# A compact attention state on the quarters of TensorE, with y sharing the scores' buffer

## The chip, the cores and the metric

The kernel runs on one core of one Trainium2 chip. The metric is the device time of one execution in microseconds (us); the median of several executions is given with its range. One run of the kernel before took 829.36 us at a granted clock of 0.849, where the ten others in its rounds took 724.08 to 726.72 us at 0.992 to 0.995; that run was in the slow state, and every run below is in the fast state unless it is marked otherwise. e1 to e4, e5 to e8 and e9 to e11 are three sets of rounds on three chips, each with its own runs of the kernel before. "Correct" means that the output was compared with the reference on the chip and agreed.

The engines are TensorE (PE in the profile; PEld are its weight loads), VectorE (DVE), ScalarE (ACT), GpSimd (POOL) and SyncE (SP), which here issues most transfers.

## The reference

A retention block (a linear attention with a decaying state) feeds a feed-forward block.

```python
# q, k, v: (4, 8, 768, 64): batch, heads, sequence, head width
gamma = 1.0 - 2.0 ** (-5.0 - np.arange(H))          # one decay for each head
for t in range(S):
    state = gamma * state + outer(k[t], v[t])       # (B, H, 64, 64)
    y[t] = (q[t] @ state) / sqrt(64)
x = y.transpose(0, 2, 1, 3).reshape(3072, 512)      # tokens x (head, width)
h = x @ w_in                                        # 512 -> 2048
out = (h * sigmoid(1.702 * h)) @ w_out              # 2048 -> 512
```

The weights come as float64. The kernel fetches them as raw 32-bit pairs and narrows them to f32 itself, on ACT and DVE, while it already computes.

## The kernel before

The sequence is cut into chunks of 128 tokens: 6 for each of 4 batch entries, 24 in all. `load` and `turn` bring q and k in and transpose them, `attend` makes the scores of a chunk and masks them, `finish` makes y and updates the state. The pieces of later chunks are woven between the dense matmuls of the feed-forward block. P is 128, H is 8 heads, HP is 4 pairs of heads, D is 64, NC is 6.

```python
state = [const.tile([P, HP, P], F32, name=f"state{i}") for i in range(2)]   # cleared at the start
...
w1v = moe_w_in.bitcast(U32).rearrange("(c p) (f two) -> p c f two", p=P, two=2)
SRC = [w1v[:, 2 * h:2 * h + 2, 2 * p * P:2 * (p + 1) * P] for p in range(NP) for h in range(2)] + ...
def fetch():                       # one transfer of 512 KB onto all 128 partitions
    ...
    sp.dma_start(x.rearrange("p (c f) two -> p c f two", c=2) if i < NFF else x, SRC[i])
...
def attend(j):
    p = ps_a.tile([P, 2, HP, P], F32, name="pa")          # ps_a: one buffer of two PSUM banks
    for hp in range(HP):
        for i in range(2):
            r = slice(i * D, (i + 1) * D)
            pe.matmul(p[:, i, hp, :], KT[j][r, hp, :], QT[j][r, hp, :], start=True, stop=True)
    for i in range(2):
        dve.tensor_mul(AT[j][:, i], p[:, i], mask[:, i])

def finish(j):
    c = j % NC
    old, new = state[c % 2], state[(c + 1) % 2]
    ...
    y = ps.tile([P, HP, P], F32, name="py", tag="att")    # "att": two buffers of one bank
    if c:
        for hp in range(HP):                              # two heads at once, block-diagonal
            pe.matmul(y[:, hp, :], old[:, hp, :], qt[:, hp, :], ...)
    for hp in range(HP):
        for i in range(2):                                # left half, right half, left, right
            pe.matmul(y[i * D:(i + 1) * D, hp, :], vn[:, 2 * hp + i, :], a[:, i, hp, :], ...)
    dve.tensor_mul(x[...], y, rowd)                       # eviction of y
    ...
    for hp in range(HP):
        pe.matmul(u[:, hp, :], kd[...], vn[...], start=True, stop=True)    # k times v of two heads
    for i in range(2):
        r = slice(i * D, (i + 1) * D)
        ...                                               # c == 0: copy
        pool.tensor_mul(new[r, :, r], old[r, :, r], cold[r, 2 * H:, None].to_broadcast([D, HP, D]))
        dve.tensor_add(new[r, :, r], new[r, :, r], u[r, :, r])
```

A state tile holds, for each pair of heads, a 128x128 matrix with one head's 64x64 state in the upper left and the other's in the lower right. The other two quarters are zero, and PE multiplies them too: the records of the state matmuls are 128*128 (L247, 1.05 us for 8 records in chunk 8).

## Time and profile before

| | before |
|---|---|
| time, median of 3 runs | 724.99 us (724.62 to 725.17) |
| span of the profiled run, mean granted clock | 722.5 us, 0.994 |
| state matmuls, all 20 chunks (groups by shape) | 14.8 + 7.6 us of PE |
| value matmuls, all 24 chunks (groups by shape) | 17.5 + 10.1 us of PE |
| from a first state start to the first value start, dense chunk | 0.984 us |

Read the engine row first: it says that PE has almost no free time. Then read the slices, which say where the little free time lies (the first two of 40, 36 us). The lines themselves stand in the prediction, with the readings that it draws from them. In the attention of one chunk, PE does scores (pa), then dense work while DVE masks them, then state and value matmuls (both into py), then the update (pu).

### The profile page before, as it was taken

The page shows a single profiled execution, that of the slowest core. Times are in us where ns is not written, and L with a number is a line of the kernel's source. Part 1 is how long each engine was busy: PE and PEld are TensorE (multiplying, and loading weights), DVE is VectorE, ACT ScalarE, POOL GpSimd, SP SyncE. Part 2 cuts the span into 40 slices and gives each one's busy share as a digit, 9 for nine tenths or more (in the row PEclk, how much of TensorE's full clock was granted, in tenths as well). Part 3 has the DMA queues.
Part 4 walks back from the last instruction along what each step waited for, and adds up shares of the span by engine and source line. Part 5 has one row for each costly group of instructions (what it writes and reads, how often), then busy time and mean ns, then how long its engine had stood idle before and what let it go on. Part 6 is the DMA issues. An engine that isn't in the chain of part 4 may idle for free.

```text
span 722.5 us, 9662 instructions
## 1 busy us (share of the span) xinstructions
PE 705.4 (98%) x3776; PEld 588.5 (81%) x3776; DVE 373.2 (52%) x542; ACT 126.7 (18%) x197; POOL 125.7 (17%) x115
## 2 busy tenths in 40 slices
PE   5799999999999999999999999999999999999997
PEld 4688885447888888888888888888888888888886
DVE  4888889993612822443743353553345373244251
ACT  2313323221000001331000332000233000133100
POOL 2241001000464403000333000123100140200030
PEclk9899999999999999999999999999999999999999
DMA  9995333420012324101334200324300320100001
GB/s 255 232 199 145 132 132 114 147 35 11 15 45 40 73 49 103 31 1 16 74 59 87 59 1 8 73 46 86 67 0 2 63 54 1 44 0 1 15 0 44
DMA packets 142765, 46.28 MB, mean 64 GB/s; under 512 B 129920, under 2 KB 136576, under 8 KB 142720
## 3 DMA queue, kind: packets, MB, share of 16 engines
q1 hardware_dynamic: 135504, 39.10, 23.8%
q10 hardware_dynamic: 7216, 6.57, 2.9%
q8 instruction: 30, 0.49, 0.3%
q14 instruction: 15, 0.12, 0.1%
HBM read 39.33 MB, written 6.29 MB: 63 GB/s over the span
## 4 chain that ended last, share of the span: by engine, by line
PE 92%; DVE 5%; DMA 1%; ACT 1%; issue 0%; SPq 0%; ACTq 0%
PE pd L403 38%; PE px L352 15%; PE py L352 11%; PE ph L313 8%; PE ph L300 7%; PE py L251 3%; PE pa L234 3%; PE pu L264 3%; PE py L247 2%; DMA q_in<-in_q_dram 1%; PE pt L217 1%; DVE W L342 1%; DVE G L342 1%; DVE W L343 1%; DVE G L343 1%; ACT W L181 0%
## 5 line engine op out<-in xcount | busy, mean ns | idle before, releaser
L403 PE MATMUL pd<-W,G 128*128 128x256 f32 x1120 | 250.3, 381 | 0.4 <-DVE G L343 0.3
L403 PEld LDWEIGHTS pd<-W,G 128*128 128x128 f32 x1120 | 210.1, 190 | 30.8 <-DVE G L343 1.2
L352 PE MATMUL px<-X,W 128*128 128x256 f32 x512 | 119.0, 379 | 0.0
L352 PEld LDWEIGHTS px<-X,W 128*128 128x128 f32 x512 | 97.3, 190 | 13.2
L352 PE MATMUL py<-X,W 128*128 128x256 f32 x384 | 90.7, 379 | 0.0
L352 PEld LDWEIGHTS py<-X,W 128*128 128x128 f32 x384 | 73.0, 190 | 9.9
L300 PE MATMUL ph<-X,W 128*128 128x256 f32 x256 | 58.2, 382 | 0.0
L225 POOL TENSOR_TENSOR kd<-kn_in,cold 128x512 f32<-128x512 f32 x13 | 13.6, 1042 | 242.0 <-PE pu L264 199.0
L313 PE MATMUL ph<-W,W 128*128 128x512 f32 x128 | 55.1, 592 | 0.0
L300 PEld LDWEIGHTS ph<-X,W 128*128 128x128 f32 x256 | 47.5, 190 | 6.7 <-DVE X L255 0.2
L313 PEld LDWEIGHTS ph<-W,W 128*128 128x128 f32 x128 | 24.3, 190 | 30.2 <-issue 29.2
L344 POOL TENSOR_TENSOR G<-G 128x512 f32<-128x512 f32 x20 | 28.9, 1444 | 113.1 <-DVE G L343 111.7
L237 DVE TENSOR_TENSOR at<-pa,mask 128x512 f32<-128x512 f32 x32 | 20.6, 684 | 45.5 <-PE pa L234 45.5
L281 DVE TENSOR_TENSOR G<-G,sg 128x512 f32<-128x512 f32 x48 | 33.0, 688 | 13.7 <-ACT sg L279 13.7
L279 ACT ACTIVATE sg<-G 128x512 f32<-128x512 f32 x48 | 30.3, 630 | 50.9 <-DVE G L362 30.6
L279 ACT ACTIVATE sg<-ph 128x512 f32<-128x512 f32 x32 | 19.1, 598 | 104.7 <-PE ph L300 56.2
L403 PE MATMUL pd<-W,W 128*128 128x256 f32 x160 | 35.6, 380 | 0.4 <-DVE W L343 0.3
L403 PEld LDWEIGHTS pd<-W,W 128*128 128x128 f32 x160 | 30.2, 190 | 5.6 <-DVE W L343 1.2
L271 POOL TENSOR_TENSOR state<-state,cold 64x256 f32<-64x256 f32 x32 | 25.6, 800 | 44.0 <-DVE state L269 24.8
L255 DVE TENSOR_TENSOR X<-py,rowd 128x512 f32<-128x512 f32 x20 | 13.8, 688 | 33.3 <-PE py L251 33.3
L390 ACT ACTIVATE u<-pd 128x512 f32<-128x512 f32 x6 | 3.6, 597 | 155.1 <-PE pd L403 155.1
L362 DVE TENSOR_TENSOR G<-py,p 128x512 f32<-128x512 f32 x16 | 11.1, 691 | 37.8 <-PE py L352 37.8
(96 smaller groups left out, 682.1 us busy)
## 6 DMA issues: line engine op xcount, KB each, us to landing
v_in<-in_v_dram SPq DMA_DIRECT2D x24, 256.0 KB, 3.9
W<-in_moe_w_in_dram SPq DMA_DIRECT2D x12, 512.0 KB, 5.1
out_dram<-o ACTq DMA_DIRECT2D x24, 256.0 KB, 2.4
kn_in<-in_k_dram SPq DMA_DIRECT2D x21, 256.0 KB, 4.1
W<-in_moe_w_out_dram SPq DMA_DIRECT2D x10, 512.0 KB, 3.7
q_sq<-in_q_dram SPq DMA_DIRECT2D x256, 16.0 KB, 1.8
k_sq<-in_k_dram SPq DMA_DIRECT2D x256, 16.0 KB, 1.8
G<-in_moe_w_out_dram SPq DMA_DIRECT2D x6, 512.0 KB, 3.8
```

The lines of the kernel that those rows point to most:

```text
L234: pe.matmul(p[:, i, hp, :], KT[j][r, hp, :], QT[j][r, hp, :], start=True, stop=True)
L237: dve.tensor_mul(AT[j][:, i], p[:, i], mask[:, i])
L251: pe.matmul(y[i * D:(i + 1) * D, hp, :], vn[:, 2 * hp + i, :], a[:, i, hp, :], start=(not c and hp == 0), stop=(hp == HP - 1), skip_group_ ...
L264: pe.matmul(u[:, hp, :], kd[:, h, :].rearrange("p i d -> p (i d)"), vn[:, h, :].rearrange("p i d -> p (i d)"), start=True, stop=True)
L271: pool.tensor_mul(new[r, :, r], old[r, :, r], cold[r, 2 * H:, None].to_broadcast([D, HP, D]))
L279: act.activation(s, h, AF.Sigmoid, scale=1.702)
L281: dve.tensor_mul(g, h[:, i], s[:, i])
L300: pe.matmul(h[:, ab], w, X[:, 2 * half + c // 2, c % 2, :], start=(ab == 0 and c == 0), stop=(c == 3), skip_group_check=True)
L313: pe.matmul(h, w, X1[:, c // 2:4:2, c % 2, :], start=(c == 0), stop=(c == 3))
L344: pool.tensor_sub(a[1], a[1], a[0])
L352: pe.matmul(acc[:, u, :], W1[:, 2 * d + u, sa, c, :], X[:, sb, c, :], start=(start and u == 0 and c == 0), stop=(stop and c == 1), skip_gr ...
L403: pe.matmul(p0[:, n, :], g1(m, p, sa)[:, n * P:(n + 1) * P], W2[:, sb, p, :], start=(new and p == 0 and n == 0), stop=(last and p == NP - ...
```

## The change

The intent: store only the 64x64 states that are not zero, so that a state tile is half as wide, and multiply each head on its own quarter of the 128x128 array, four heads at a time. y then lies in two banks of PSUM (the memory that TensorE writes its results to), one for each half of the array's rows. That two banks are needed for this is not shown: no run here lets both row halves write one bank. y takes the buffer of the scores, in turn with them. Three things follow. The heads that share a partition half of y change, so the rows of the first weight are needed in another order, and each of its fetches becomes two, one for each half of the partitions. The value matmuls come in another order. The decay of a state becomes one GpSimd instruction instead of two.

```diff
-    state = [const.tile([P, HP, P], F32, name=f"state{i}") for i in range(2)]
+    state = [const.tile([P, HP, D], F32, name=f"state{i}") for i in range(2)]
...
-    w1v = moe_w_in.bitcast(U32).rearrange("(c p) (f two) -> p c f two", p=P, two=2)
+    w1v = moe_w_in.bitcast(U32).rearrange("(o c r d) (f two) -> c r d o f two", o=2, c=2, d=D, two=2)
...
-    SRC = [w1v[:, 2 * h:2 * h + 2, 2 * p * P:2 * (p + 1) * P] for p in range(NP) for h in range(2)] \
+    SRC = [[w1v[c, h, :, :, 2 * p * P:2 * (p + 1) * P] for c in range(2)] for p in range(NP) for h in range(2)] \
...
-            sp.dma_start(x.rearrange("p (c f) two -> p c f two", c=2) if i < NFF else x, SRC[i])
+            if i < NFF:
+                for c in range(2):
+                    sp.dma_start(x[c * D:(c + 1) * D].rearrange("p (o f) two -> p o f two", o=2), SRC[i][c])
+            else:
+                sp.dma_start(x, SRC[i])
...
-        p = ps_a.tile([P, 2, HP, P], F32, name="pa")
+        p = ps_a.tile([P, 2, HP, P], F32, name="pa", tag="pa")
...
-        y = ps.tile([P, HP, P], F32, name="py", tag="att")
+        y = ps_a.tile([P, 2, HP, P], F32, name="py", tag="pa")
+        where = [(y[s % 2 * D:(s % 2 + 1) * D, r, s // 2, :], s, r) for s in range(HP) for r in range(2)]
         if c:
-            for hp in range(HP):
-                pe.matmul(y[:, hp, :], old[:, hp, :], qt[:, hp, :], start=(hp == 0), stop=False,
-                          skip_group_check=True)
-        for hp in range(HP):
-            for i in range(2):
-                pe.matmul(y[i * D:(i + 1) * D, hp, :], vn[:, 2 * hp + i, :], a[:, i, hp, :],
-                          start=(not c and hp == 0), stop=(hp == HP - 1), skip_group_check=True)
+            for out, s, r in where:
+                k = slice(r * D, (r + 1) * D)
+                pe.matmul(out, old[k, s, :], qt[k, s, :], start=(s < 2), stop=False, skip_group_check=True)
+        for out, s, r in where:
+            pe.matmul(out, vn[:, 2 * s + r, :], a[:, r, s, :], start=(not c and s < 2), stop=(s >= 2),
+                      skip_group_check=True)
...
+        if c:
+            pool.tensor_mul(new, old, cold[:, 2 * H:, None].to_broadcast([P, HP, D]))
         for i in range(2):
             r = slice(i * D, (i + 1) * D)
             if c == 0:
-                dve.tensor_copy(new[r, :, r], u[r, :, r])
+                dve.tensor_copy(new[r], u[r, :, r])
             else:
-                pool.tensor_mul(new[r, :, r], old[r, :, r],
-                                cold[r, 2 * H:, None].to_broadcast([D, HP, D]))
-                dve.tensor_add(new[r, :, r], new[r, :, r], u[r, :, r])
+                dve.tensor_add(new[r], new[r], u[r, :, r])
...
-    for t in state:
-        dve.memset(t, 0.0)
```

The cuts leave out only the eviction's new slices and the loads of the row decays in the new order.

More of the change, by code (lines that the diff above doesn't have):

```diff
@@ L243, in finish @@
         vn, a, qt = QKV.pop(("v", j)), AT.pop(j), QT.pop(j)
-        y = ps.tile([P, HP, P], F32, name="py", tag="att")
+        y = ps_a.tile([P, 2, HP, P], F32, name="py", tag="pa")
+        where = [(y[s % 2 * D:(s % 2 + 1) * D, r, s // 2, :], s, r) for s in range(HP) for r in range(2)]
         if c:
-            for hp in range(HP):
-                pe.matmul(y[:, hp, :], old[:, hp, :], qt[:, hp, :], start=(hp == 0), stop=False,
-                          skip_group_check=True)
-        for hp in range(HP):
-            for i in range(2):
-                pe.matmul(y[i * D:(i + 1) * D, hp, :], vn[:, 2 * hp + i, :], a[:, i, hp, :],
-                          start=(not c and hp == 0), stop=(hp == HP - 1), skip_group_check=True)
+            for out, s, r in where:
[4 more added lines that the diff above has]
+                      skip_group_check=True)
         half, t0 = divmod(j % CB * P, TH)
         x = X1 if j // CB == 1 else X
-        dve.tensor_mul(x[:, 2 * half:2 * half + 2, :, t0:t0 + P].rearrange("p s c t -> p (s c) t"), y, rowd)
+        dve.tensor_mul(x[:, 2 * half:2 * half + 2, :, t0:t0 + P], y[:, :, 0:2, :],
+                       rowd.rearrange("p (r o) t -> p r o t", r=2))
         if j + 2 < 2 * CB:
@@ L435 @@
     act.dma_start(cold, col_decay)
-    for s in range(2):
-        act.dma_start(
-            rowd[s * D:(s + 1) * D],
-            bass.AP(tensor=row_decay.tensor, offset=row_decay.offset + s * P,
-                    ap=[[0, D], [2 * P, HP], [1, P]]),
-        )
+    for c in range(2):
+        for r in range(2):
+            act.dma_start(
+                rowd[c * D:(c + 1) * D, 2 * r:2 * r + 2],
+                bass.AP(tensor=row_decay.tensor, offset=row_decay.offset + (2 * c + r) * P,
+                        ap=[[0, D], [4 * P, 2], [1, P]]))
     load(0)
```

## The prediction

> **What bounds the kernel now.** I read the engine table and the 40 slices first, then the chain that ended last, then the groups by shape, and then the timeline around one chunk of the attention (a chunk is 128 tokens of one batch entry; there are 24).
>
> ```profile
> span 722.5 us, 9662 instructions
> PE 705.4 (98%) x3776; PEld 588.5 (81%) x3776; DVE 373.2 (52%) x542; ACT 126.7 (18%) x197; POOL 125.7 (17%) x115
> PE   5799999999999999999999999999999999999997
> PE 92%; DVE 5%; DMA 1%; ACT 1%; issue 0%; SPq 0%; ACTq 0%
> ```
>
> TensorE (PE) is busy in 98% of the span and carries 92% of the chain that ended last. Only the first two slices (36 us) have room. From about 47 us on, everything that takes time out of PE's stream takes it out of the whole, and everything off PE counts only where PE waits for it. DVE and POOL, at 52% and 17%, are no bound.
>
> The timeline of PE around chunk 8, in the middle of a dense stage (columns: start us, length us, engine, line, what, shapes, count):
>
> ```profile
> 225.28 1.16 PE L234 MATMUL pa<-qT,kT 64*128 64x128 f32 x16
> 226.37 3.72 PE L403 MATMUL pd<-W,G 128*128 128x256 f32 x16
> 229.93 1.05 PE L247 MATMUL py<-qT,state 128*128 128x128 f32 x8
> 230.92 1.09 PE L251 MATMUL py<-at,v_in 128*64 128x128 f32 x16
> 231.94 1.16 PE L264 MATMUL pu<-v_in,kd 128*128 128x128 f32 x8
> 232.94 1.25 PE L403 MATMUL pd<-W,G 128*128 128x256 f32 x5
> ```
>
> Each f32 matmul of the program leaves two records, so the 4 state matmuls (L247) are 8 records. Their pace: the group lasts 1.05 us, one record 275 ns (median), so (1.05 - 0.275)/7 = 0.111 us from start to start. The scores (L234) and the value matmuls (L251), which fill half the array each, have 16 records in 1.16 and 1.09 us: twice as many in the same time. The record starts show why: two of them, in different halves, start 7 ns apart, and such pairs follow each other at 109 to 112 ns. So halves do run side by side.
>
> The record starts also show what a change of shape costs. Dense to scores: 310 ns between the last dense start and the first score, against 216 ns between dense records, so 94 ns extra. State to value: 205 ns instead of 112, and 160 ns instead of 109 after the first pair, so 93 + 51 = 144 ns extra. Dense to state costs nothing (216 ns, both are 128*128).
>
> [...]93 to 94 ns extra at a change, pairs 7 ns apart. [...]no run here has shown four quarters at once yet. [...]the second record of the first matmul starts about 0.2 us (at the start of a group) or 0.1 us after the first record of the second matmul.
>
> **The change part by part.**
>
> 1. State matmuls. Removed: 4 of 128*128 per chunk, half of whose weights are zeros of the block-diagonal state (8 records). Added: 8 of 64*64, on four quarters in turn (16 records). From the first state start to the first value start is now 0.984 us in every dense chunk. After, if quarters run four at a time as halves run two at a time: four rounds. The first waits for its mode change, the second comes 0.160 us later (I take the 64-column value group as model), the third and fourth 0.109 us later each, and the value group 0.205 us after that: 0.160 + 0.109 + 0.109 + 0.205 = 0.583 us. Before it there is now a mode change: +0.094 us. Saved per chunk: 0.984 - 0.583 - 0.094 = 0.307 us. There are 20 chunks with a state (24 less the 4 first ones of a sequence).
>
> 2. A new wait. y moves into the buffer of the scores (one buffer of two banks), so the state matmuls can no longer start before DVE has read both halves of the scores. Before, only the value matmuls waited for that. I compared, per chunk, the end of the second mask multiplication (L237) with the first state start. In 12 of the 20 there is slack (0.38 us in one, over 2.1 us in ten, 3.5 us in chunk 1). In 8 there is none:
>
> ```profile
> 74.34 1.27 DVE L237 TENSOR_TENSOR G<-pa,mask 128x512 f32<-128x512 f32 x2
> 74.91 1.05 PE L247 MATMUL py<-G,state 128*128 128x128 f32 x8
> 75.89 1.09 PE L251 MATMUL py<-G,v_in 128*64 128x128 f32 x16
> ...
> 243.50 1.28 DVE L237 TENSOR_TENSOR at<-pa,mask 128x512 f32<-128x512 f32 x2
> 244.59 1.05 PE L247 MATMUL py<-qT,state 128*128 128x128 f32 x8
> 245.57 1.09 PE L251 MATMUL py<-at,v_in 128*64 128x128 f32 x16
> ```
>
> Chunk 5 (above): the mask ends at 75.61, 0.70 us after the state group began. With 0.05 us to release, the state starts at 75.66 and the value group at 75.66 + 0.583 = 76.24 instead of 75.89: 0.35 us lost. Chunk 7 (0.47 us short): 0.12 lost. Chunks 9, 13, 17, 21 (0.19 us short each; 9 is shown): value group at 244.78 + 0.05 + 0.583 = 245.41 instead of 245.57: still 0.15 saved each. Chunks 2 and 3 (0.13 and 0.37 short): 0.30 and 0.06 saved. Chunk 1 lies at 24 to 28 us, where DVE's weight conversion ends later than PE's work: I count 0.
>
> Sum: 11 chunks x 0.307 = 3.4; 4 x 0.15 = 0.6; chunks 2 and 3, 0.36; chunks 5 and 7, -0.47. Together 3.9 us saved.
>
> 3. Value matmuls. Their number and shape stay, their order changes: from left half, right half, left, right to left, left, right, right. If PE can pass a waiting matmul of the busy half, nothing changes. If it stops at the head of its queue, 8 matmuls need 5 slots of two records instead of 4: about 2 x 0.109 = 0.22 us more per chunk, over 24 chunks 5.2 us.
>
> 4. Off the path. POOL decays the state with one 128x256 instruction instead of two of 64x256 (32 took 25.6 us; by the number of columns I expect half), DVE's eviction of y keeps its 512 elements a partition (0.69 us), two clears of 0.49 us go. The next scores now wait for the eviction of y; its end lies 0.28 us ahead of the next scores in chunk 0 and over 3 us in all others. All of that is hidden.
>
> 5. Transfers. Each of the 16 fetches of the first weight is two of half the size. Only in the first 30 us do they matter, where queued loads wait for earlier ones; the bytes are the same. I allow 1 us either way.
>
> **The rivals.**
>
> A. The value matmuls lose their pairing (part 3): 3.9 saved less 5.2 lost, about 726.[...] Against it: in the trace the second matmul does start ahead of the first one's second record. I give it 0.3.
>
> B. Quarters run only two at a time: eight rounds, 0.160 + 6 x 0.109 + 0.205 = 1.02 us plus 0.094, so 0.13 us lost per chunk instead of 0.307 saved. With the waits of part 2 some 4 to 5 us lost, about 729. For it: nothing in this trace has four at once. Against it: row halves and column halves each pair here. I give it 0.1.
>
> C. The new wait for the buffer takes more than part 2 says, because DVE's order shifts, or the start of the kernel, where DVE is full, gets longer: 724 to 726. The order of instructions of the changed program keeps the mask multiplications, evictions and conversions in their places, against it. I give it 0.1.
>
> D. All is hidden or gained as written: 721.1.
>
> **The range.** The main line gives 725.0 - 3.9 = 721.1. Weighing A, B and C in, I move the prediction to 722.0, with 718.8 to 727.0 as the range. Two per cent are 14.5 us. The state matmuls, all told, take 14.8 + 7.6 = 22.4 us of PE in the groups by shape; even halving them would not give 14.5 us, and no rival loses as much. So within 2% has 0.97, faster 0.01, slower 0.02.
>
> **What would show it.** Part 1: 16 state records on quarters in about 0.65 us, four starting within some 25 ns, and 0.58 us from the first state start to the first value start in chunks with slack (0.98 before). If two at a time, 1.0 us. Part 2: PE idle ahead of the state group, released by the mask multiplication, in chunks 5, 7, 9, 13, 17, 21 and nowhere else after 50 us. Part 3: the value group of chunk 8 lasts 1.02 us to the next group; 1.24 would be rival A. Part 4: POOL's state line at about 13 us in all. Part 5: the first dense matmuls still begin at about 29 us. The prediction fails if either pairing assumption is wrong, or if the first 50 us move by more than 1 us.

## The result, and the profile after

The changed kernel is correct and takes 726.2 us (median of 4 runs, 725.46 to 727.38), against 725.08 us for the kernel before in the same rounds (4 runs, 724.62 to 727.03). The ratio is 1.0012, with a 95% interval of 0.9989 to 1.0035: the same by the 2% rule. In a later set of rounds it took 726.3 us (5 runs) against 725.86 us (9 runs), ratio 1.0008 (0.9994 to 1.0022). A ratio here is the mean time of one kernel's fast runs over the mean of the other's in the same rounds, so it is not quite the ratio of the medians quoted beside it. The range of the prediction held, but its main line (a gain of 3.9 us) did not come: there is no gain at all.

The engine table, the slices of PE and the chain that ended last, in the page of the changed kernel:

```profile
span 724.9 us, 9986 instructions
PE 701.1 (97%) x3936; PEld 578.3 (80%) x3936; DVE 371.6 (51%) x540; ACT 126.9 (18%) x197; POOL 110.3 (15%) x99
PE   5599999999999999999999999999999999999997
PE 76%; DVE 10%; SPq 7%; DMA 4%; issue 2%; ACT 1%; POOL 0%; ACTq 0%; DVEq 0%
```

PE is busy for 4.3 us less than before (705.4 to 701.1), and the span is still 2.3 us longer (722.54 to 724.88): PE stands idle for 6.7 us more. The second slice, 7 before and 5 now, says where to look: at the start. The chain has lost 16 points of PE, but that is not a new bound. At chunk 9 PE now waits 0.17 us for a mask, and the chain goes off there through DVE into the loads that DVE waited for long before; all that time PE was busy. In e6 and e7 below, where that wait is gone, the chain is PE's again, with 91% and 90%.

The timeline of PE around chunk 8 (start us, length us, engine, line, what, shapes, count), then around chunk 9, where the brackets show the idle time ahead of a group and what ended it:

```profile
229.80 1.16 PE L239 MATMUL pa<-qT,kT 64*128 64x128 f32 x16
230.89 3.72 PE L411 MATMUL pd<-W,G 128*128 128x256 f32 x16
234.54 0.67 PE L256 MATMUL py<-qT,state 64*64 64x128 f32 x16
235.14 1.14 PE L258 MATMUL py<-at,v_in 128*64 128x128 f32 x16
236.21 1.16 PE L272 MATMUL pu<-v_in,kd 128*128 128x128 f32 x8
```

```profile
249.19 0.67 PE L256 MATMUL py<-qT,state 64*64 64x128 f32 x16 [0.17 <-DVE at L242]
249.79 1.15 PE L258 MATMUL py<-at,v_in 128*64 128x128 f32 x16
250.86 1.16 PE L272 MATMUL pu<-v_in,kd 128*128 128x128 f32 x8
```

The state group is down from 1.05 to 0.67 us with twice as many records: four quarters do run at once. The next two things are small and new. The value group takes 1.14 to 1.15 us instead of 1.09, and 1.07 us pass from its start to the start of the update, instead of 1.02. And chunk 9 waits for DVE.

The timeline of PE in the start, first of the kernel before, then of the changed one (the transposes pt are those of q of chunk 2, the state group is chunk 1's, ph are the first dense matmuls):

```profile
16.01 1.16 PE L234 MATMUL pa<-G 64*128 64x128 f32 x16
21.57 1.09 PE L217 MATMUL pt<-ident,q_in 128*128 128x128 f32 x4 [4.41 <-DMA q_in<-in_q_dram]
24.25 2.08 PE L247 MATMUL py<-G,state 128*128 128x128 f32 x8 [0.46 <-ACT G L218]
...
29.32 3.72 PE L300 MATMUL ph<-X,W 128*128 128x256 f32 x16
```

```profile
17.38 1.16 PE L239 MATMUL pa<-G 64*128 64x128 f32 x16
26.79 1.12 PE L222 MATMUL pt<-ident,q_in 128*128 128x128 f32 x4 [8.24 <-DMA q_in<-in_q_dram]
...
33.93 3.62 PE L308 MATMUL ph<-X,W 128*128 128x256 f32 x16
```

Chunk 1's scores end within 1.4 us of where they ended before; then PE waits 8.24 us for q of chunk 2 instead of 4.41. The load of q is the same. It was issued later (17.80 us instead of 12.98), because it stands in the queue behind the fetches of the first weight, and the dense matmuls begin 4.6 us later.

The same place as the transfers see it. In the transfer view of the first 60 us, GB/s is what was moved in each of 40 slices of 1.5 us. The line under it is the fetches of the first weight: how many, KB each, median us from issue to landing. First the kernel before, then the changed one:

```profile
GB/s 0 126 255 184 214 336 237 219 316 385 389 391 351 233 300 286 215 228 243 4 8 242 395 286 218 218 217 169 0 106 355 338 254 166 166 177 370 176 0 0
...
W<-in_moe_w_in_dram SPq DMA_DIRECT2D x10, 512.0 KB, 5.1
```

```profile
GB/s 0 155 247 208 219 229 206 218 220 223 234 243 232 239 240 222 206 203 194 214 204 229 185 186 239 249 220 197 143 148 3 0 87 258 232 203 208 202 113 258
...
W<-in_moe_w_in_dram SPq DMA_DIRECT2D x20, 256.0 KB, 6.5
```

From 13.5 to 18 us the kernel before moves 385 to 391 GB/s. The changed one never gets over 258. Half as many bytes take longer to land (6.5 us instead of 5.1). In the records of single packets, a 2 KB packet of these fetches took 84 to 87 ns (median) before and 142 to 147 ns after.

The whole balance, from the starts of the state groups in the two traces:

| stretch of the span | before, us | after, us | change |
|---|---|---|---|
| start to the state matmuls of chunk 4 | 59.38 | 63.65 | +4.27 |
| chunk 4 to chunk 8 | 170.55 | 170.89 | +0.34 |
| chunk 8 to chunk 23 (dense) | 382.02 | 379.92 | -2.10 |
| chunk 23 to the end | 110.59 | 110.42 | -0.17 |
| span | 722.54 | 724.88 | +2.34 |

So the matmuls gained, but less than predicted, and the start lost more than that. Nothing was "hidden": the two cancel.

### The profile page after: what moved, and what is told of

Read it like the earlier page. It is cut to its first block, busy times and chain, and to the rows that moved or that the text cites. A ratio compares the mean times of both kernels' runs of the same rounds, so it can differ in the third digit from the quotient of the medians.

```text
span 724.9 us, 9986 instructions
## 1 busy us (share of the span) xinstructions
PE 701.1 (97%) x3936; PEld 578.3 (80%) x3936; DVE 371.6 (51%) x540; ACT 126.9 (18%) x197; POOL 110.3 (15%) x99
## 4 chain that ended last, share of the span: by engine, by line
PE 76%; DVE 10%; SPq 7%; DMA 4%; issue 2%; ACT 1%; POOL 0%; ACTq 0%; DVEq 0%
PE pd L411 27%; PE px L360 15%; PE py L360 11%; PE ph L321 8%; SPq L125 6%; PE ph L308 6%; PE py L258 3%; PE pu L272 2%; DVE G L350 2%; PE pa L239 2%; PE py L256 2%; DMA kn_in<-in_k_dram 1%; DVE G L351 1%; DVE G L349 1%; DMA k_sq<-in_k_dram 1%
## 5 line engine op out<-in xcount | busy, mean ns | idle before, releaser
L384 DVE TENSOR_TENSOR G<-py,vv 128x512 f32<-128x512 f32 x16 | 11.1, 692 | 25.7 <-ACT vv L381 25.7
```

## The experiments

My theory after this reading: the start is longer because a transfer onto half of the partitions runs slower, and the dense chunks gain less because the new order of the value matmuls costs 0.05 us a chunk and the wait for the mask costs four chunks their gain. Rivals: the start is longer because there are twice as many transfers, or because of a lower granted clock in the start, or because of the new sharing of the buffer there; and the dense chunks lose by something else than order and wait.

A table of all runs first. "Chunk 4" is the start of its state matmuls, which closes the start; "packet" is the median of the first weight's 2 KB packets; the third column counts the timed runs.

| run | what it is | runs | time, us | ratio to before (95%) | chunk 4, us | packet, ns |
|---|---|---|---|---|---|---|
| e1 | after, fetch cut by columns | 5 | 835.98 | 1.153 (1.1509 to 1.1551) | 139.43 | 84 |
| e2 | after, single fetch, wrong | 6 | 727.2 | 1.0012 (0.9987 to 1.0037) | 60.39 | 84 to 85 |
| e3 | before, fetch in partition halves | 6 | 728.94 | 1.0051 (1.0034 to 1.0069) | 63.24 | 142 to 146 |
| e4 | after, value matmuls alternating | 5 | 724.48 | 0.999 (0.9974 to 1.0006) | 62.41 | |
| e5 | after, heads permuted, single fetch | 6 | 723.41 | 0.9972 (0.9956 to 0.9988) | 59.77 | 84 |
| e6 | after, y in banks of its own | 5 | 723.85 | 0.9981 (0.9966 to 0.9997) | 62.69 | |
| e7 | e4, e5 and e6 together | 5 | 719.41 | 0.9919 (0.9904 to 0.9935) | 58.55 | 84 |
| e8 | e2 again, one run (state unknown), wrong on purpose | 1 | 726.9 | | 63.67 | |
| e9 | before, fetch cut by columns | 5 | 724.96 | 0.999 (0.9975 to 1.0005) | 58.89 | 84 |
| e10 | before, fetch in even and odd partitions | 4 | 752.25 | 1.0365 (1.0349 to 1.0381) | 85.26 | 84 |
| e11 | after again | 5 | 726.3 | 1.0008 (0.9994 to 1.0022) | 63.29 | 142 |

The kernel before had medians of 725.39 (e1 to e4, 11 runs), 725.46 (e5 to e8, 10 runs) and 725.86 us (e9 to e11, 9 runs). An eleventh run beside e5 to e8 took 829.36 us at a clock of 0.849 and isn't used. All runs but e2 and e8 gave correct outputs.

### The start: how the weight is fetched

**e3_before_half_fetch** puts nothing but the halved fetch into the kernel before.

```diff
-            sp.dma_start(x.rearrange("p (c f) two -> p c f two", c=2) if i < NFF else x, SRC[i])
+            if i < NFF:
+                for c in range(2):
+                    r = slice(c * D, (c + 1) * D)
+                    sp.dma_start(x[r].rearrange("p (c f) two -> p c f two", c=2), SRC[i][r])
+            else:
+                sp.dma_start(x, SRC[i])
```

> The kernel before with its fetches of the first weight cut by partition halves as in the changed one, all else as before; right result. Theory (rate of half-partition transfers): packets near 147 ns, the state of chunk 4 near 63.9 us instead of 59.4, the time about 729.5. Rival (the loss at the start belongs to the attention, not to the fetch): about 725, chunk 4 at 59.4.

It costs 0.51% (728.94 us), which is 3.7 us of 725.4. Chunk 4 comes 3.86 us later than in the kernel before (63.24 instead of 59.38), of the 4.27 us that the whole change lost there. Everything else in this kernel is as before, so the fetch alone makes some nine tenths of the loss in the start.

**e9_before_columns** keeps the number of transfers of e3, but cuts each fetch along its columns, so that both parts go onto all 128 partitions.

```diff
+                for c in range(2):
+                    sp.dma_start(x[:, c * 2 * P:(c + 1) * 2 * P], SRC[i][:, c])
```

> The kernel before with each fetch of the first weight cut in two by columns: 128 partitions, one run of 2 KB each, so as many transfers and packets as in e3; right result. If the half of the partitions costs the rate: packets near 86 ns, chunk 4's state near 59.4 us, 725. If it is the number of transfers: packets near 146 ns or chunk 4 late, 729.

The transfer view of the first 60 us, first of e3, then of e9 (slices of 1.5 us, then fetches, KB each, median us to landing):

```profile
GB/s 0 130 242 198 234 227 187 219 222 232 234 249 235 238 250 223 201 211 225 185 219 209 153 238 242 227 221 198 149 144 2 15 234 249 206 174 217 193 225 234
...
W<-in_moe_w_in_dram SPq DMA_DIRECT2D x20, 256.0 KB, 6.4
```

```profile
GB/s 0 123 237 223 233 333 228 219 321 382 367 358 344 253 247 307 227 243 254 12 45 299 276 255 218 198 247 201 15 229 332 216 232 53 194 253 340 259 0 0
...
W<-in_moe_w_in_dram SPq DMA_DIRECT2D x20, 256.0 KB, 4.5
```

Both have 20 fetches of 256 KB in the window. On half of the partitions they stay at 250 GB/s or below, on all of them they reach 382; a fetch lands after 6.4 us or after 4.5. The time of e9 is the time of the kernel before (ratio 0.999). The number of transfers is not the cause, and the rival falls. It does have a part in when q is issued: in e9 the load of q for chunk 2 goes out at 15.50 us, 2.5 us later than before, but PE gets it at 22.04 us, hardly later than before (21.57).

**e10_before_even_odd** asked whether it is 64 partitions, whichever they are, or a half that lies together: `r = slice(c, P, 2)` in place of the slice of e3.

> The kernel before with each fetch cut in two by even and odd partitions: 64 partitions each as in e3, but spread over all 128; right result. If it matters which partitions (one contiguous half): packets near 86 ns, 725. If 64 rows are too few, wherever they lie: packets near 146 ns, 729.

The packets answer: 84 ns on every other partition, so 64 rows are not slow as such. Nor were there fewer of them at once: while the weight is fetched, 12.2 of its packets are in flight on average, against 13.1 in e3, and in the same view of the first 60 us the rate reaches 359 GB/s:

```profile
GB/s 0 123 240 230 246 326 220 211 345 359 356 358 354 255 53 170 5 0 178 160 27 163 191 251 245 18 68 307 149 105 70 30 322 266 81 0 238 247 214 0
```

The time (752.25 us) answers nothing, and as a test of time the run is a miss. In the waits of the first 62 us, ScalarE's eviction of a transpose waits for a transfer of the weight (line, what it waited for: us in total, times, longest):

```profile
ACT L223 <- DMA G<-in_moe_w_in_dram: 20.5, 1, 20.5
```

The transfer and the eviction write different columns of one tile, so by the columns the data doesn't need the wait; what put it in is not shown. Chunk 4 comes 26 us later in this run.

**e1_fetch_by_columns** tried to mend the changed kernel as e9 cuts the kernel before.

```diff
-    SRC = [[w1v[c, h, :, :, 2 * p * P:2 * (p + 1) * P] for c in range(2)] for p in range(NP) for h in range(2)] \
+    SRC = [[w1v[:, h, :, o, 2 * p * P:2 * (p + 1) * P] for o in range(2)] for p in range(NP) for h in range(2)] \
...
-                for c in range(2):
-                    sp.dma_start(x[c * D:(c + 1) * D].rearrange("p (o f) two -> p o f two", o=2), SRC[i][c])
+                for o in range(2):
+                    sp.dma_start(x[:, o * 2 * P:(o + 1) * 2 * P], SRC[i][o])
```

> The changed kernel, but each pair of fetches of the first weight is cut by columns (128 partitions, one 2 KB run each) and no longer by partitions (64 partitions, two runs each). Same bytes, same number of transfers, right result. Theory, the loss at the start is the rate of transfers that write half the partitions: 2 KB packets fall from about 147 ns (median) back to about 86 ns, the state of chunk 4 starts near 59.3 us instead of 63.65, the time is about 721.7. Rival, the number of transfers[...]: packets and chunk 4 stay, the time is about 726.

A miss: 835.98 us. The packets were fast (84 ns), but only two were in flight at a time (exactly two in 89% of the fetch time, against some 13 before), and the rate fell to 51 GB/s. With the rows in the new order, the source's outermost size here is 2 (the halves), where that of e9 and of the kernel before is 128. No run varies it alone, so that it is the cause is not shown.

**e5_heads_permuted** avoids the question: it permutes the heads when q and k are loaded, so that the rows of the weight keep their blocks of 128 and one transfer does for a fetch. Loads of q and k in the first eight chunks become two each, and the decay table is permuted to match.

```diff
+    def head(s, r):
+        return 4 * (s % 2) + 2 * r + s // 2
...
-            sp.dma_start(QKV[name, j], src[b, :, rows, :].rearrange("h p d -> p h d"))
... (v stays as it was; for q and k:)
+                for c2 in range(2):
+                    sp.dma_start(QKV[name, j][:, 4 * c2:4 * c2 + 4],
+                                 src[b, c2:H:2, rows, :].rearrange("h p d -> p h d"))
...
-    w1v = moe_w_in.bitcast(U32).rearrange("(o c r d) (f two) -> c r d o f two", o=2, c=2, d=D, two=2)
+    w1v = moe_w_in.bitcast(U32).rearrange("(o r p) (f two) -> r p o f two", o=2, r=2, two=2)
... (the places of y, the value's heads, the decays and the later loads follow the permutation)
```

> The changed kernel with the heads put in another order at the loads of q and k (two transfers each instead of one), so that the first weight can again be fetched in one transfer over all 128 partitions; right result. Theory (the rate of half-partition transfers is the loss at the start): 2 KB packets near 86 ns, the state of chunk 8 starts near 231.5 us as in e2 (234.5 in the changed kernel), the time 722 to 724. Rival (e2's slow runs show that something else holds the start, such as the clock of TensorE at half after its wait for q): packets near 86 ns all the same, and most runs near 727 us.

Correct, packets at 84 ns, chunk 4 at 59.77 us instead of 63.65, and 723.41 us: 0.28% faster than the kernel before. So undoing the halves in the changed kernel (e5) gives back at chunk 4 what adding them to the kernel before (e3) took: 3.88 and 3.86 us. By chunk 8 it is 3.07 us, because chunk 5 now waits longer for its mask: the gap ahead of its state group is 1.63 us, against 0.82 in the changed kernel.

### The start: the clock

**e2_fetch_whole_wrong** is the changed kernel with the single fetch of before. The rows of the weight are then in the wrong order and the output is wrong (relative error 1.2); the work is the same.

```diff
-    w1v = moe_w_in.bitcast(U32).rearrange("(o c r d) (f two) -> c r d o f two", o=2, c=2, d=D, two=2)
+    w1v = moe_w_in.bitcast(U32).rearrange("(c p) (f two) -> p c f two", p=P, two=2)
... (SRC and the transfer as in the kernel before)
```

> The changed kernel with the one fetch per half weight of the kernel before (128 partitions, two runs). The rows of the first weight then lie in the wrong order, so the result is wrong on purpose. Both theories: the start is as quick as before, chunk 4 near 59.3 us, the time about 721.7. Together with e1: what e2 gains over e1 is the price of the number of transfers; the rate theory says under 0.7 us, the rival about 4.5 us. If neither gains, the loss at the start is that of the attention's new waits.

The six times fall into two groups: 723.03 and 723.62, and 727.08 to 728.03. The profiled run was one of the fast ones (chunk 4 at 60.39 us). The median of 727.2 taken alone would say that the fetch doesn't matter, against e3, so I ran the same kernel again.

**e8_fetch_whole_again** has no edit against e2. It took 726.9 us, so the profile shows the other group.

> The kernel of e2 once more for its profile, as e2's runs fell into two groups (723.0 and 723.6 against 727.1 to 728.0) and the profile was of the quick one. Wrong result on purpose. If the run is a slow one: chunk 8's state starts near 235.5 us, and the half clock of TensorE lasts longer at the start (10 us instead of 3.4). If the groups are of something later, chunk 8 starts near 231.5 all the same.

The first dense group in the timeline of PE, e2 first, then e8:

```profile
30.16 3.72 PE L307 MATMUL ph<-X,W 128*128 128x256 f32 x16 [3.21 <-DVE X L261]
```

```profile
30.54 6.61 PE L307 MATMUL ph<-X,W 128*128 128x256 f32 x16 [3.18 <-DVE X L261]
```

The same kernel, the same idle time ahead (3.2 us), and the same 16 records take 3.72 us in one and 6.61 us in the other. The records of the granted clock agree: in e2 the clock was at half from 21.4 to 24.8 us only; in e8 from 22.8 to 26.2 us and again from 29.6 to 36.4 us.

In the traces, the recorded stretches at one clock are multiples of 3.41 us, but for each trace's last, and they lie differently against the start of the span (the first record is at 14.43 us before and at 16.59 in the changed kernel). Split into windows of 3.41 us, they show that the window ahead of a fall need not be idle. In e8 the clock fell at 29.6 us, after a window with 1.17 us of PE work; in e2 the same idle time fell into two windows with 2.14 and 1.49 us of work, and the clock stayed. Between the first record and the last change of the 13 traces, 30 windows at full clock were followed by half clock, none with more than 1.50 us of PE work, and 2630 were not, none with less than 1.48. In e2 and e8 the same idle time fell differently into the windows, and the clock fell ahead of the dense matmuls in e8 alone; why it falls no run shows.

e2's runs have two outcomes about 4 us apart (3.3 us in the two profiles), and its median says only which came more often. The kernel before has them too: its 18 fast runs at a granted clock of 0.994 or more have a median of 724.8 us, the other 12 one of 726.5. Why four of e2's six runs were slow ones and none of e5's six was not asked.

The time at half clock, counted from the first record of the clock (at 14 to 17 us in these traces), was 6.8 us before, 6.8 in e3 and 10.3 in the profiled run of the changed kernel; the profiles of e3 and before compare at equal time at half clock, and that is why the loss by halves rests on e3 and not on e2. The clock is also a rival for the changed kernel itself, since e8, with the single fetch, comes to chunk 4 as late as it does. But the two lose at different places. In e8 the dense matmuls begin at 30.54 us and then run slowly. In the changed kernel the half clock ends at 33.7 us, before its dense matmuls begin (33.93), and these take 3.62 us, no longer than in e2 at full clock (3.72); its delay was there by 26.79 us, in the wait for q.

### The dense chunks: order and wait

**e4_value_alternating** sorts the value matmuls so that left and right halves alternate again.

```diff
-        for out, s, r in where:
+        for out, s, r in sorted(where, key=lambda w: (w[1] // 2, w[2], w[1])):
             pe.matmul(out, vn[:, 2 * s + r, :], a[:, r, s, :], start=(not c and s < 2), stop=(s >= 2),
```

> The changed kernel with the value matmuls in an order that alternates the two column halves again; right result. The group takes 1.074 us to the next group in the changed kernel and 1.024 before. If the order is the cause: 1.024 again in all 24 chunks, 24 x 0.05 = 1.2 us less in all, about 725.0. If the change of mode ahead of it is the cause: 1.074 stays, about 726.2.

The timeline of PE at chunk 8 in e4:

```profile
233.70 1.09 PE L258 MATMUL py<-at,v_in 128*64 128x128 f32 x16
234.73 1.16 PE L272 MATMUL pu<-v_in,kd 128*128 128x128 f32 x8
```

The group lasts 1.09 us again, and its start to the next group's is back at 1.024 us by the record starts (1.074 in the changed kernel). From chunk 8 to 23 PE takes 379.18 us instead of 379.92: 0.74 us for 15 chunks is 0.05 a chunk, the difference of the groups. In the whole that is 1.2 us, and the measured gain (1.0012 to 0.999, 1.6 us) contains it. The edit also makes the partners of a pair write the same bank again, as before, where the changed kernel switches banks from one matmul to the next; so it is the order that costs, but halves and banks are not told apart.

**e6_y_own_banks** takes the new wait away: from chunk 4 on y gets two banks of its own (the two single-bank buffers), and the update u takes the scores' buffer in exchange. The eviction of y becomes two instructions.

```diff
-        y = ps_a.tile([P, 2, HP, P], F32, name="py", tag="pa")
-        where = [(y[s % 2 * D:(s % 2 + 1) * D, r, s // 2, :], s, r) for s in range(HP) for r in range(2)]
+        if j < CB:
+            yy = ps_a.tile([P, 2, HP, P], F32, name="py", tag="pa")
+            y = [yy[:, r] for r in range(2)]
+        else:
+            y = [ps.tile([P, HP, P], F32, name=f"py{r}", tag="att") for r in range(2)]
+        where = [(y[r][s % 2 * D:(s % 2 + 1) * D, s // 2, :], s, r) for s in range(HP) for r in range(2)]
...
-        u = ps.tile([P, HP, P], F32, name="pu", tag="att")
+        if j < CB:
+            u = ps.tile([P, HP, P], F32, name="pu", tag="att")
+        else:
+            u = ps_a.tile([P, 2, HP, P], F32, name="pu", tag="pa")[:, 0]
```

> The changed kernel with y out of the scores' buffer from chunk 4 on: y in the two banks of the transposes, the new state's product in the scores' buffer instead; right result. If the shared buffer makes the state matmuls wait for the mask: the gap ahead of the state group falls to 0.309 us in chunks 5, 7, 9, 13, 17 and 21 (from 0.82 in two and 0.55 in four), 2 x 0.51 + 4 x 0.24 = 2.0 us less, about 724.2. If not, the gaps stay, about 726.2. A loss would be that the next scores wait for the update of the state.

The gap ahead of the state group is 0.309 us in every chunk from 4 on, where the changed kernel has 0.545 to 0.556 us in chunks 9, 13, 17 and 21 and 0.82 us in 5 and 7. From chunk 8 to 23 it takes 378.96 us, 0.96 less than the changed kernel: four chunks by 0.24 us. From chunk 4 to 8 it takes 169.87 us, 1.02 less: two chunks by 0.51. So the waits are what cost those chunks their gain. The time is 723.85 us, 0.19% faster than the kernel before.

**e7_heads_alt_own** has the edits of e4, e5 and e6 together.

> e5, e4 and e6 together (heads in another order, value matmuls alternating, y in banks of its own); right result. Theory: the gains add, 726.2 - 3 (start) - 1.2 - 2.0 = 720.0, first state of chunk 8 to that of chunk 23 about 377.5 us (382.0 before, 379.9 changed). If the start keeps its slow mode as in e2: 723 to 724.

The span and the timeline of PE at chunk 9, where the changed kernel waited:

```profile
span 717.3 us, 10032 instructions
```

```profile
243.05 0.67 PE L264 MATMUL py<-qT,state 64*64 64x128 f32 x16
243.65 1.09 PE L266 MATMUL py<-at,v_in 128*64 128x128 f32 x16
244.67 1.16 PE L287 MATMUL pu<-v_in,kd 128*128 128x128 f32 x8
```

It is correct and takes 719.41 us (719.03 to 720.02), ratio 0.9919 (0.9904 to 0.9935): 0.8% faster than the kernel before, and the best version here, though still "same" by the 2% rule. No bracket stands at chunk 9 any more, and the value group is at 1.09 us. From chunk 8 to 23 it takes 378.20 us, which is what e4 and e6 gave apart (379.92 - 0.74 - 0.96); the 377.5 that I expected was added up wrongly. Against the changed kernel the three edits gave 0.22, 0.40 and 0.31% apart (1.0012 less 0.999, 0.9972 and 0.9981), 0.93% in sum, and 0.93% together. The three come from different rounds and each has an interval of some 0.15% either way; within that they add up, as three separate losses would. They are not wholly separate: the wait at chunk 5 grows when the start gets shorter (e5).

**e11_after_again** ran the changed kernel in the rounds of e9 and e10.

> The changed kernel as it is, in the same rounds as e9 and e10, to have it beside more runs of the kernel before: 726.2, 1.0012 times the time before. Chunk 8 to chunk 23 takes 379.9 us again, chunk 4's state starts near 63.6 us again.

It took 726.3 us, with chunk 4 at 63.29 us and packets at 142 ns; the first measurement stands.

## Why the prediction was right or wrong, point by point

The range held, and so did the class. That the range held was in part luck: it was wide because of rivals A and C (726, and 724 to 726), and what filled it was a loss in the start by another cause than either named. The point of 722.0 us was 4.2 us low, because the main line's 3.9 us did not come out. Compared stretch by stretch, the main line expected -0.2 us up to chunk 8 (-0.30 - 0.06 - 0.31 + 0.35 + 0.12), -3.36 from chunk 8 to 23 (9 chunks x 0.307 and 4 x 0.15) and -0.3 in chunk 23. The traces have +4.6, -2.1 and -0.2. Of the 6.2 us between them, 4.8 arose before chunk 8, 1.3 in the dense chunks and 0.1 at the end.

1. **Quarters: right.** Four state records start 7 ns apart, ahead of the second record of the first, and rounds follow at 160, 109 and 109 ns, as assumed; the value group follows after 220 ns, where 205 was put. First state start to first value start is 0.598 us (0.583 predicted, 0.984 before), and the gap ahead 0.309 us (0.310 worked out from 216 and 94 ns). In the groups by shape the state matmuls went from 22.4 to 9.3 + 4.5 = 13.8 us. Rival B (two at a time) falls.

2. **The new wait: right in kind, its release mis-sized.** PE waits for the mask in chunks 5, 7, 9, 13, 17 and 21, as named, and in 2 and 3, which were counted as short too. From the end of the mask to the first state start it took 0.15 us, where I had put 0.05 (the trace before has 0.055 us from the end of DVE's eviction, L255, at 29.266 us to the first dense matmul, L300, at 29.321). Chunks 9, 13, 17 and 21 therefore gain 0.007 us at most instead of 0.15, and chunks 5 and 7 lose 0.27 each instead of 0.35 and 0.12.

3. **The value matmuls: neither main line nor rival A.** The reversed order costs 0.05 us a chunk, where the main line has 0 and rival A 0.22 (an estimate, one slot more of 2 x 0.109 us; the trace before showed nothing for it): 1.2 us over 24 chunks instead of 5.2. Whatever PE does with the waiting matmul of a busy half, it is not a whole slot; e4 shows that the order is the cause (1.024 us again). The record starts of chunk 8 show where the 0.05 us arise: before, two partners start 7 ns apart all along; in the changed kernel 13 ns apart in the first five pairs and 57 ns apart in the last three, so the last record starts 0.05 us later. A chunk with the full gain thus nets 0.242 us, not 0.307. With 9 such chunks, 4 of point 2 and 2 without a state, which only lose 0.05, the stretch from 8 to 23 should gain 9 x 0.242 + 4 x 0.007 - 2 x 0.05 = 2.11 us; the trace has 2.10.

4. **Off the path: right.** POOL's line, the last one below, is at half, and evictions stayed ahead of the next scores. In the groups of the changed kernel (line, engine, out and in, shapes, count, busy us and mean ns, idle before):

```profile
L275 POOL TENSOR_TENSOR state<-state,cold 128x256 f32<-128x256 f32 x16 | 12.6, 788 | 53.3 <-DVE state L281 35.5 <-DVE state L279 17.8
```

5. **Transfers: the step that failed.** The prediction put it: "the bytes are the same. I allow 1 us either way." They are the same bytes, but not at the same rate. Packets of the first weight took 142 to 147 ns instead of 84 to 87, the fetches held up q of chunk 2, and chunk 4 came 4.27 us late; e3 shows 3.86 us for this alone at the same time at half clock. The test that the prediction set itself, "the first dense matmuls still begin at about 29 us", failed (33.93), and so did its condition that the first 50 us move by no more than 1 us. The profile before had shown that the start was a queue of transfers at up to 391 GB/s, and one line of the diff, the slice of 64 partitions, was enough to ask. Other runs agree: at most 250 GB/s in e3 against 382 in e9 and 391 before, and every other partition (e10) at full packet speed (84 ns). These rates also hold the loads of q, k and v, which go onto all partitions. Why one half takes less is not shown by any run here.

Rival C had the start in it, but by DVE or the buffer. What lengthened it was the queue of transfers, and DVE only waited in its turn.

The +0.34 us from chunk 4 to 8 is accounted for by points 1 to 3: from the start of chunk 4's state to that of chunk 8's, chunk 4 saves 0.34 us, chunks 5 and 7 lose 0.27 each, chunk 6 loses 0.05, and the change of shape ahead of chunk 8 takes 0.09.

What stays open: the remaining 0.4 us of the start (4.27 less 3.86). I suspect the longer half clock (chunk 1's update took 1.78 us at 32.31 us, against 1.16 before), but no run separates it. It is also no more than executions (and chips) differ by: the same kernel comes to chunk 4 at 63.28 us in e11, and e6, whose edit takes effect only from chunk 4 on, at 62.69. Why partners drift apart within the value group isn't shown either.

## What to carry to other kernels

A change that packs the array better also decides where data must lie, and the transfers that put it there belong in the sum: transfers onto one half of the partitions, 0 to 63 or 64 to 127, moved at most 258 GB/s here where whole ones moved up to 391, with the same bytes and packets. Before choosing an order of heads or rows, look for the permutation that leaves every transfer on all partitions (e5: packets at 84 ns, 128 outermost in the source; e1, with 2 outermost, fell to 51 GB/s), keep alternate halves of the array in turn (e4: 1.024 us a group instead of 1.074), and don't let two stages share a buffer only because its size fits (e6: 0.24 us for each of four chunks, 0.51 for each of two): the three together turned no gain into one of 0.8%. In e2, with 3.2 us of idle PE ahead of the first dense matmuls, the times lay in two groups some 4 us apart, so compare profiles at equal clock and not medians alone.
